# An attention-plus-MLP kernel: the hand-written call order of its first four chunks replaced by one in which products and evictions are listed separately

## The chip, the cores and the metric

One core of one Trainium2 chip runs the whole program. The metric is the device time of one execution in microseconds, the median of several runs. A profile of one execution gives a row for every instruction of the five engines: TensorE (PE in the rows, its weight loads PEld), VectorE (DVE), ScalarE (ACT), GpSimd (POOL) and the queue that issues transfers (SP).

## The reference

```python
# q, k, v: (4, 8, 768, 64); sort_net: (4, 8, 8, 8); w_in: (512, 2048); w_out: (2048, 512)
P = sort_net
for _ in range(5):
    P = exp(P - max(P, -1)); P = P / sum(P, -1); P = P / sum(P, -2)
k_sorted = einsum('bhij,bhjcd->bhicd', P, k_blocks)      # 8 blocks of 96 rows
v_sorted = einsum('bhij,bhjcd->bhicd', P, v_blocks)
s = q_blocks @ k_sorted^T / 8
attn = softmax(s) @ v_sorted                             # per block of 96 queries
x = attn reshaped to (3072, 512)
h = x @ w_in
out = (h * cos(h)) @ w_out                               # (3072, 512) float32
```

## The kernel before

All matrix operands are bfloat16, PSUM and the output float32. Each engine works through its own instruction list in order, so the order in which the Python calls are made is the schedule: it is written out by hand, call by call.

**Chunks and units.** The 3072 tokens are eight chunks `n` of 384 tokens. A chunk is four units `u` of 96 queries, one block of one batch element with its eight heads. Chunks 0 to 3 belong to the first group of two batch elements, 4 to 7 to the second.

**The head.** The five rounds of normalisation (`rounds`) run on DVE and ACT. Two small products (`block`) turn the result into matrices `bds[0]` and `bdv` (`spread`, DVE) that mix the key and value rows. `kp` makes sorted keys of the first batch element in PSUM tiles of 16 column steps, and `k_place` moves them to `kTs`, `half=0` for the blocks of chunk 0 and `half=1` for those of chunk 1. `kxp` (POOL) copies keys of chunk 1 to the other rows. `v_permute` (POOL) reorders value columns, `v0` makes eight of the 64 sorted value columns, `v0e` moves them to `vS[0]`.

**A unit of attention.** `s_ps` scores on PE, `s_max` and `s_sub` on DVE, `expo` the exponential on ACT, `p_ps` the transpose of the probabilities on PE with its eviction `p_ev`, `av_products` on PE, `av_norm` on DVE (a reciprocal and a multiplication), `x_ps` the transpose of the result on PE and its eviction `x_ev` to `xT`. From chunk 2 on the scores are `qk_half`, `qk` or a `batch`, and part of the transposes are DMAs on the SP queue.

**The MLP.** `up` makes two of the 16 blocks of h (eight products of 384 columns), ACT takes the cosine, DVE multiplies. `down` accumulates 16 products of 512 columns to 128 output rows. Chunk 0 does this in half chunks and quarters: `up_four(h, g, part)` needs only units 0 and 1 for `h=0` and 2 and 3 for `h=1`; `cos_four`, `gate_four`, and `down_four(ts, q)`.

**Other work in between.** `ks`/`kse` sort the keys of batch element 1, `v_sort_b` its values (64 columns in eight calls), `k_sort_g` and `v_sort_g` those of the second group (into `kT2` and `vS[1]`, which lies in `pair`), `q_products`/`q_place_half` transpose the queries.

**Buffers that tie the lists together.** PSUM holds three tiles named `big` of two banks and two named `acc` of one, taken in turn; a product waits until the tile three (or two) allocations back has been evicted. Every large load goes through the one queue that POOL issues: `load`, `load_pair`, `load_q`, `load_w_in`, `load_w_out`.

`keep_warm` puts out products of zeros on PE, as `fill=` of some calls as well. The calls of before, in the first stretch, joined to lines:

```python
kp(2, *B); kp(0, *B); v_permute x4; k_place(2, A, 1); k_place(2, V, 0); kp(1, *B); k_place(0, A, 0)
blocks.append(block(...)); k_place(1, V, 0); k_place(1, A, 1); values_matrix(); k_place(0, A, 1)
s_ps(0, 0, fill=3); v0(4, *C); s_max(0, 0); v0(0, *B); v0e(4, A); s_sub(0, 0); s_ps(0, 3); ...
```

Units of chunk 0 come in the order 0, 3, 1, 2, those of chunk 1 in the order 1, 0, 3, 2. All eight `v_sort_b` of batch element 1 stand between the eight `up` of chunk 1.

Of the kernel before, what the change touches and what calls it, by code (L numbers as in the profile page):

```python
# [18 lines left out]
def kernel(  # L19
# [15 lines left out]
    nc = tc.nc  # L35
# [214 lines left out]
    keep_warm(14, big.tile([128, 512], FP32, name="idle", tag="big"))  # L250
# [80 lines left out]
    def idle(times):  # L331
        keep_warm(times, big.tile([128, 512], FP32, name="idle", tag="big"))
# [64 lines left out]
    blocks = [block([pick[:]])]  # L397
    spread(bds[0], blocks[0], xs=slice(H, 2 * H))

    def values_matrix():  # L400
        spread(bdv, blocks[1], xs=slice(0, H))
        spread(bds[0], blocks[0], xs=slice(0, H))
        spread(bdv, blocks[1], xs=slice(H, 2 * H))
# [197 lines left out]
    def p_hold(n, u):  # L601
        hold(pT[n, u])
# [14 lines left out]
    def av_products(n, u, fill=0):  # L617
# [5 lines left out]
        pt = pT.pop((n, u)).rearrange("p a c -> p (a c)")  # L623
# [123 lines left out]
    def kp(t, pool, tag, fill=0):  # L747
        o = ps["k", t] = pool.tile([128, 16, 2 * NB], FP32, name="ks", tag=tag)
        keep_warm(fill, o[:, :8].rearrange("p t n -> p (t n)"))
        for z in range(16):  # L750
            k_products(o, z, t * 16 + z, slice(0, 128),
                       bds[0][:, H:].rearrange("p x i -> p (x i)"))

    def k_place(t, eng, half=None):
        lo, hi = (0, nb) if half is None else (half * IC, half * IC + IC)
        o = ps["k", t]
        copy_on(
            eng, kT[0].rearrange("p z (h i) t -> p z h i t", i=nb)[
                :, ::2, :, lo:hi, t * 16:t * 16 + 16],
# [134 lines left out]
    wz = iter(range(40, D, 4))  # L894
    kz = iter(range(6, 12))

    def k_next():
        k_sort_g(next(kz) * 4, A, *C)

    def w_next(eng=A, pool=None, tag="acc"):  # L900
        v_sort_g(next(wz), 4, eng, pool or acc, tag)

    kp(2, *B)
    kp(0, *B)
    v_permute(slice(0, 64), 32, False, 8, 40)
    v_permute(slice(0, 64), 40, False, 8, 48)
    v_permute(slice(0, 64), 48, False, 8, 56)
    v_permute(slice(0, 64), 56, False, 8, 64)
    k_place(2, A, 1)
    k_place(2, V, 0)  # L910
    kp(1, *B)
    k_place(0, A, 0)
    blocks.append(block([pick[:, :, z * PB:(z + 1) * PB] for z in (1, 0)]))
    k_place(1, V, 0)
    k_place(1, A, 1)
    values_matrix()
    k_place(0, A, 1)
    s_ps(0, 0, fill=3)
    v0(4, *C)
    s_max(0, 0)  # L920
    v0(0, *B)
    v0e(4, A)
    s_sub(0, 0)
    s_ps(0, 3)
    v0e(0, A)
    v0(5, *C)
    s_max(0, 3)
    load_w_out(0)
    v0e(5, A)
    s_ps(0, 1)  # L930
    load_w_out(1)
    load_w_out(2)
    load_w_out(3)
    v0(6, *C)
    ones(0)
    expo(0, 0, True)
    s_ps(0, 2)
    s_sub(0, 3)
    v0(1, *C)
    v0e(6, A)  # L940
    s_max(0, 1)
    expo(0, 3, True)
    v0(3, *B, fill=2)
    s_sub(0, 1)
    v0e(1, A)
    p_ps(0, 0, *C, fill=2)
    v0e(3, A)
    s_max(0, 2)
    v0(7, *C)
    expo(0, 1, True)  # L950
    kxp(2)
    v0(2, *B, fill=1)
    p_ev(0, 0, V)
    v0e(7, A)
    s_sub(0, 2)
    kxp(0)
    p_ps(0, 1, *C)
    v0e(2, A)
    p_ps(0, 3, *C)
    p_ev(0, 1, V)  # L960
    expo(0, 2, True)
    kxp(1)
    av_products(0, 0)
    z_turned(1)
    av_norm(0, 0, True)
    av_products(0, 1)
    p_ev(0, 3, A)
    p_ps(0, 2, *C)
    av_norm(0, 1, True)
    x_ps(0, 0, *B)  # L970
    load(kbuf, 0, kin_d[1])
    p_ev(0, 2, A)
    load(vbuf, 64, vin_d[1])
    picks(pick_pair, (2, 3))
    av_products(0, 3, fill=2)
    av_norm(0, 3, True)
    x_ps(0, 1, *C)
    x_ev(0, 0, A)
    av_products(0, 2)
    q_products(1, 0, 0, 16, *C)  # L980
    x_ev(0, 1, A)
    av_norm(0, 2, True)
    x_ps(0, 3, *B)
    q_place_half(1, 0, 1, A)
    up_four(0, 0, 0)
    z_vperm()
    up_four(0, 0, 1)
# [267 lines left out]
```

## Time and profile before

| | |
|---|---|
| median of 3 runs | 232.1 us (231.99 to 232.11) |
| the profiled execution's own time | 231.61 us |
| its span, first to last instruction | 229.8 us |
| PE busy | 220.8 us (96%) |
| DVE busy | 170.8 us (74%) |
| ACT busy | 154.4 us (67%) |
| POOL busy | 96.1 us (42%) |

The span leaves 1.8 us of the execution outside. Busy time of PE is not PE at its peak: products are pipelined, and a row lasts longer than the distance to the next. The chain of work that ended last, in order of time, gives the distance.

### The profile page before, as it was taken

How to read it: one execution, taken by the hardware profiler on the slowest of the kernel's cores; microseconds unless marked ns; L12 is line 12 of the kernel's file. 1: busy time of each engine (PE TensorE's matmuls, PEld its weight loads, DVE VectorE, ACT ScalarE, POOL GpSimd, SP SyncE). 2: the span in 40 equal slices, each digit the busy share in tenths (PEclk: the TensorE clock that was granted, in tenths of full speed). 3: DMA queues.
4: the chain of work that ended last, by engine and by line, in shares of the span. 5: the costliest groups of instructions: out<-in, count | busy, mean ns of one | idle time of the engine just before them, and what ended most of it. 6: DMA issues, size and time to landing. Idle time of an engine off the chain costs nothing.

```text
span 229.8 us, 5513 instructions
## 1 busy us (share of the span) xinstructions
PE 220.8 (96%) x2245; PEld 138.7 (60%) x2268; DVE 170.8 (74%) x291; ACT 154.4 (67%) x207; POOL 96.1 (42%) x121
## 2 busy tenths in 40 slices
PE   8788999999999999999999999999999999999994
PEld 3378898567765566655665456655655565556554
DVE  6769968978698778868489977987699769646700
ACT  5659877777889858797688466736674667716521
POOL 7999999399950197943609000800000000000000
PEclk9999999999999999999999999999999999999999
DMA  6999999994999799667979939964924440351012
GB/s 83 225 187 207 202 206 236 195 227 148 124 124 191 171 139 148 118 135 146 162 118 163 135 74 148 210 98 81 206 92 80 90 160 0 69 147 46 0 46 94
DMA packets 67833, 31.21 MB, mean 136 GB/s; under 512 B 56416, under 2 KB 63200, under 8 KB 67552
## 3 DMA queue, kind: packets, MB, share of 16 engines
q0 software_dynamic: 24048, 13.64, 43.3%
q1 hardware_dynamic: 43472, 17.02, 35.1%
q8 instruction: 18, 0.29, 0.5%
q10 hardware_dynamic: 288, 0.20, 0.3%
q14 instruction: 7, 0.06, 0.1%
HBM read 27.27 MB, written 6.29 MB: 146 GB/s over the span
## 4 chain that ended last, share of the span: by engine, by line
PE 90%; DVE 3%; POOL 2%; issue 1%; ACT 1%; POOLq 0%; ACTq 0%
PE h L672 32%; PE o L697 30%; PE h L860 5%; PE o L881 4%; PE av L628 4%; PE sc L441 3%; PE ks L408 2%; PE o L1219 2%; PE pps L838 1%; PE sc L507 1%; PE xps L659 1%; PE vs L785 1%; PE vs L452 1%; PE qps L268 1%; PE xps L847 1%
## 5 line engine op out<-in xcount | busy, mean ns | idle before, releaser
L672 PE MATMUL h<-xT,w_in_t 128*128 128x384 bf16 x448 | 78.4, 326 | 0.1
L697 PE MATMUL o<-w_out_t,gg 128*128 128x512 bf16 x303 | 73.7, 379 | 1.0 <-issue 0.3
L676 ACT ACTIVATE c<-h,half_pi 128x768 f32<-128x768 f32 x56 | 50.5, 902 | 26.0 <-PE h L672 25.0
L680 DVE TENSOR_TENSOR gg<-c,h 128x768 bf16<-128x768 f32 x56 | 52.7, 949 | 19.5 <-ACT c L676 19.5
L672 PEld LDWEIGHTS <-w_in_t 128*128 128x128 bf16 x448 | 42.2, 98 | 26.3 <-DVE xT L259 0.6
L697 PEld LDWEIGHTS <-gg 128*128 128x128 bf16 x320 | 29.0, 99 | 28.3
L573 ACT ACTIVATE p_buf<-s 96x768 bf16<-96x768 f32 x32 | 26.6, 843 | 5.2 <-DVE s L494 4.0
L179 POOL COPY vperm<-kv 64x768 bf16<-64x768 bf16 (+2 forms) x12 | 28.4, 2416 | 3.9 <-DMA kv<-in_v_dram 3.9
L494 DVE TENSOR_TENSOR s<-sc,mx 96x384 f32<-96x384 f32 (+1 forms) x33 | 24.3, 735 | 1.6
L492 DVE TENSOR_REDUCE mx<-sc 96x4 f32<-96x384 f32 (+1 forms) x33 | 24.0, 729 | 0.2 <-PE sc L507 0.2
L641 DVE TENSOR_TENSOR xn<-av,r 96x512 bf16<-96x512 f32 x32 | 22.0, 687 | 1.1
L129 POOL DMA_DIRECT2D kv<-in_q_dram x24 | 16.0, 676 | 0.7 <-issue 0.7
L257 ACT COPY kv<-o 128x512 f32<-128x512 f32 (+2 forms) x10 | 5.2, 524 | 14.1 <-PE o L697 11.5
L257 ACT CAST kTs<-ks 128x512 bf16<-128x512 f32 (+1 forms) x18 | 11.0, 630 | 5.3 <-PE ks L408 4.4
L639 DVE RECIPROCAL r<-av 96x8 f32<-96x8 f32 x32 | 6.4, 199 | 9.6 <-PE av L628 9.1
L129 POOL DMA_DIRECT2D q_mem<-in_q_dram x16 | 10.7, 687 | 2.0 <-DMA kv<-in_v_dram 1.5
L881 PE MATMUL o<-w_out_t,gg 128*128 128x512 bf16 x45 | 11.2, 379 | 0.2
L259 DVE COPY kv<-o 128x512 f32<-128x512 f32 (+1 forms) x5 | 3.1, 612 | 11.1 <-PE o L1219 8.5
L860 PE MATMUL h<-xT,w_in_t 128*128 128x192 bf16 x128 | 11.1, 246 | 0.0
L441 PE MATMUL sc<-kTs,q_turned 128*128 128x96 bf16 x152 | 11.1, 206 | 0.0
L599 POOL CAST held<-q_turned 96x1 f32<-96x1 bf16 x2 | 0.4, 184 | 24.3 <-DMA q_turned<-q_mem 16.3
L860 PEld LDWEIGHTS <-w_in_t 128*128 128x128 bf16 x128 | 10.5, 98 | 0.0
(134 smaller groups left out, 285.6 us busy)
## 6 DMA issues: line engine op xcount, KB each, us to landing
out_dram<-kv SPq DMA_DIRECT2D x12, 256.0 KB, 2.7
out_dram<-o_s SPq DMA_DIRECT2D x10, 256.0 KB, 3.5
w_in_t<-in_moe_w_in_dram POOLq DMA_DIRECT2D x4, 512.0 KB, 11.7
w_out_t<-in_moe_w_out_dram POOLq DMA_DIRECT2D x4, 512.0 KB, 12.3
kv<-in_k_dram POOLq DMA_DIRECT2D x2, 768.0 KB, 9.8
kv<-in_v_dram POOLq DMA_DIRECT2D x2, 768.0 KB, 12.9
pair<-in_k_dram POOLq DMA_DIRECT2D x2, 768.0 KB, 12.3
kv<-in_v_dram POOLq DMA_DIRECT2D x6, 256.0 KB, 5.3
```

The source lines that it names most:

```text
L129: nc.gpsimd.dma_start(out=q_heads[:, i, :, e], in_=src[:, ih * IC + i, :, e])
L179: nc.gpsimd.tensor_copy(dst, src)
L492: nc.vector.reduce_max(mx[:], scv, axis=AX.X)
L494: nc.vector.tensor_tensor(s, scv, mx.to_broadcast(list(s.shape)), op=ALU.subtract)
L573: nc.scalar.activation(p[:, :, :blk], s_t.pop((n, u)).rearrange("p e h c -> p (e h) c"), AF.Exp, scale=scale)
L641: nc.vector.tensor_tensor(xn.rearrange("p h e d -> p e h d"), avv[:, :, :, :D], r.to_broadcast([blk, 2, H2, D]), op=ALU.mult)
L672: nc.tensor.matmul(h[:, f2, :w], w_in_t[:, kk, f * 128:(f + 1) * 128], xT[n][:, kk], start=(kk == 0), stop=(kk == KC - 1))
L676: nc.scalar.activation(c[:], h[:, :, :w], AF.Sin, bias=half_pi[:, 0:1])
L680: nc.vector.tensor_tensor(gt[n, fp // 2][:, f:f + 2], c[:], h[:, :, :w], op=ALU.mult)
L697: nc.tensor.matmul(o[:], gt[n, f // 4][:, f % 4, ts * 128:(ts + 1) * 128], w_out_t[:, f, :], start=(f == 0), stop=(f == FC - 1))
L860: nc.tensor.matmul(o[:, part, f2 * w:(f2 + 1) * w], w_in_t[:, kk, f * 128:(f + 1) * 128], xT[0][:, kk, h * w:(h + 1) * w], start=(kk == 0) ...
L881: nc.tensor.matmul(out_ps[ts][:], gt[0, q][:, f % 4, ts * 128:(ts + 1) * 128], w_out_t[:, f, :], start=(f == 0), stop=(f == FC - 1))
```

## The change

The calls from the first keys to the output layer of chunk 3 are listed anew. What was one call with a product and its eviction becomes two, so that each engine's list has an order of its own: `uh`/`uc`/`ug` for `up`, `dn`/`dc` for `down` (in quarters), `qs`/`qr` and `qs2`/`qr2` for `qk_half` and `qk`, `bt`/`be` for `batch`, `xp`/`xe`, `kg`/`kge`, `vg`/`vge`, `vb`/`vbe`. The instructions are the same, but for three things: the first keys are made in four PSUM tiles (columns 16 to 24, 32 to 48, 0 to 16, 24 to 32) instead of three; the ones beside the values are set by DVE instead of POOL; the zero products have 256 columns instead of 512, twice as many of those in `idle` and at the start, and other `fill` counts in between.

The units of chunk 0 come in the order 0, 1, 2, 3, those of chunk 1 in the order 2, 3, 1, 0. Several evictions change engine.

```diff
-    keep_warm(14, big.tile([128, 512], FP32, name="idle", tag="big"))
+    keep_warm(28, big.tile([128, 512], FP32, name="idle", tag="big"), 256)
...
-    blocks = [block([pick[:]])]
+    blocks = [block([pick[:]]), block([pick[:, :, z * PB:(z + 1) * PB] for z in (1, 0)])]
     spread(bds[0], blocks[0], xs=slice(H, 2 * H))
...
+    nc.vector.memset(vS[0][:, :, D:D + 1], 1.0)
...
-    def kp(t, pool, tag, fill=0):
-        o = ps["k", t] = pool.tile([128, 16, 2 * NB], FP32, name="ks", tag=tag)
+    def kp(c, n, pool, tag, fill=0):
+        o = ps["k", c] = pool.tile([128, n, 2 * NB], FP32, name="ks", tag=tag)
...
+    def uh(n, fp):
+        h = ps["h", n, fp] = big.tile([128, 2, 512], FP32, name="h", tag="big")
...
+    def uc(n, fp):
+        c = ps["c", n, fp] = cosp.tile([128, 2, TC], FP32, name="c", tag="c")
...
+    def vb(b, d0, nd, pool, tag):
+        o = ps["vb", b, d0] = pool.tile([128, nd, 2 * NB], FP32, name="vs", tag=tag)
...
+    def vbe(b, d0, nd, eng):
+        copy_on(
+            eng, vS[0][:, b * 2 * NB:(b + 1) * 2 * NB, d0:d0 + nd],
+            ps.pop(("vb", b, d0))[:blk].rearrange("p t n -> p n t"))
...
+    def dn(n, ts, q):
+        if q == 0:
+            out_ps[n, ts] = acc.tile([128, Dm], FP32, name="o", tag="acc")
...
```

The new list, calls joined to lines (B is a `big` tile, C an `acc` tile, V is DVE, A is ACT), from the first keys to chunk 1's first `uh`:

```python
kp(16, 8, *B); k_place(16, A, 0); kp(32, 16, *B); k_place(32, V, 0); kp(0, 16, *B)
v_permute(40..48); k_place(16, A, 1); k_place(0, A, 0); v_permute(48..56); kp(24, 8, *C)
k_place(24, V, 0); k_place(24, V, 1); v0(0, *C); v_permute(32..40); s_ps(0, 0); k_place(32, A, 1)
k_place(0, A, 1); v0e(0, A); kxp(0); v0(5, *B); v0e(5, A); v0(2, *C); s_max(0, 0); s_sub(0, 0)
s_ps(0, 1); v0(6, *C); s_max(0, 1); v0e(2, A); v0e(6, A); s_ps(0, 2); s_ps(0, 3); expo(0, 0)
s_max(0, 2); v0(3, *C); v0e(3, A); v_permute(56..64); p_ps(0, 0, *C, fill=1); v0(1, *C); s_sub(0, 1)
picks(pick_pair); p_ev(0, 0, A); s_max(0, 3); expo(0, 1); v0e(1, A); v0(4, *C); v0e(4, A)
v0(7, *B, fill=1); v0e(7, A); p_ps(0, 1, *C, fill=1); load(vbuf); s_sub(0, 2); s_sub(0, 3)
z_turned(1); load(kbuf); load_w_out(0); av_products(0, 0, fill=2); p_ev(0, 1, V)
av_products(0, 1, fill=1); av_norm(0, 0); expo(0, 2); p_ps(0, 2, *B); last = block([pick_pair[:]], *C)
av_norm(0, 1); expo(0, 3); p_ps(0, 3, *B); p_ev(0, 3, V); load_w_out(1); kxp(1); p_ev(0, 2, A)
x_ps(0, 0, *C); x_ps(0, 1, *B); x_ev(0, 1, V); kxp(2); av_products(0, 2, fill=1); load_w_out(2)
x_ev(0, 0, A); av_products(0, 3); av_norm(0, 2); spread(bds[1], last); up_four(0, 3, 0) ...
x_ps(0, 2) ... up_four(0, 1) ... x_ps(0, 3); q_products(1, 0); q_products(1, 1) ... up_four(0, 0)
up_four(0, 2) ... up_four(1, 1) ... ks(4, *C); up_four(1, 0) ... s_ps(1, 2); ks(0, *C); up_four(1, 2)
down_four(0, 0); s_ps(1, 3); down_four(2, 0); up_four(1, 3); down_four(0, 1) ... down_four(2, 3)
down_out(0, A); s_max(1, 0); down_out(2, A); s_sub(1, 0); kse(5, V); ks(1, *B); kse(1, V)
vb(1, 8, 8, *C); vbe(.., A); p_ps(1, 2, *B); ks(2, *C); p_ev(1, 2, V); vb(1, 32, 8, *B); vbe(.., V)
vb(1, 24, 8, *B); p_ps(1, 3, *C); p_ev(1, 3, V); p_ps(1, 1, *B); kse(2, A); vbe(24, A); vb(1, 48, 8, *C)
ks(3, *B); vb(1, 56, 8, *C); expo(1, 0); p_ev(1, 1, V); av_products(1, 2); vbe(48, A); av_norm(1, 2)
kse(3, A); p_ps(1, 0, *B); p_ev(1, 0, V); down_four(1, 0); av_products(1, 3); av_norm(1, 3); kg(16, *B)
av_products(1, 0); av_norm(1, 0); kge(16, A); down_four(1, 1); x_ps(1, 2, *B); down_four(1, 2)
x_ev(1, 2, A); vbe(56, V); av_products(1, 1); x_ps(1, 0, *B); down_four(1, 3); x_ev(1, 0, A)
x_ps(1, 3, *B); av_norm(1, 1); vb(1, 40, 8, *C); down_out(1, V); x_ps(1, 1, *B); x_ev(1, 3, A)
vbe(40, V); x_ev(1, 1, A); vb(1, 16, 8, *B); vbe(16, V); q_products(2, 0, *B); q_products(2, 1, *B)
q_place_half(2, 0, 0, V); q_place_half(2, 1, 0, V); uh(1, 4); uc(1, 4) ...
```

After that the list goes on in the same manner to the end of chunk 3's `dn`; `kg(24)` and `kg(40)` now stand between the `uh` of chunk 1, the loads of the second group's values and queries are issued earlier, and nothing is changed from the transposes of `q` for chunk 6 on.

838 lines of the change are left out of this document (566 added, 272 removed).

## Prediction

> **What bounds the kernel now.** I read the page first, then PE's busy time by stretches, then the chain of work that ended last in order of time, then the waits and the engines' rows in the stretch where the chain leaves PE.
>
> ```profile
> span 229.8 us, 5513 instructions
> PE 220.8 (96%) x2245; PEld 138.7 (60%) x2268; DVE 170.8 (74%) x291; ACT 154.4 (67%) x207; POOL 96.1 (42%) x121
> ```
>
> ```profile
> 12.05:27.75 15.70, 14.31 (x302) 1.00 1.23 201
> 27.75:56.40 28.65, 28.49 (x395) 1.00 1.04 207
> 56.40:84.06 27.66, 27.45 (x309) 1.00 0.99 146
> ```
>
> (Stretch, its length, PE busy and instructions, granted clock, DMA share, GB/s.) 96% alone would not prove it, because a product's row outlasts the distance to the next. The chain, which counts from start to start, does (start, length, what):
>
> ```profile
> 12.09 0.36 PE bl L386 x8
> 12.75 1.56 PE ks L408 x48
> 14.31 0.51 PE bl L386 x16
> 14.82 0.34 PE sc L246
> 15.59 0.35 PE sc L804 x16
> 15.96 0.96 DVE mx L824
> 19.49 0.84 PE vs L785 x8
> 20.34 0.22 PE vs L246
> 26.98 0.50 PE qps L268 x16
> 27.75 3.30 PE h L860 x40
> 48.36 0.36 PE pps L838 x8
> 48.72 0.26 PE av L628 x8
> 50.47 0.17 PE xps L847 x4
> 52.12 0.86 PE o L881 x4
> 58.28 1.30 PE h L672 x8
> 59.59 0.25 PE vs L452 x8
> 205.82 10.40 PE h L672 x64
> ```
>
> Eight `h` products take 1.30 us at 58.28 and 64 take 10.40 at 205.82: 0.1625 us each in both, whatever lies between. From 27.75 us on, PE runs at one rate, and the two stretches leave it 0.16 and 0.21 us idle. All the products there stay in the new list, so after 27.75 nothing can be won but some 0.3 us; it can only be lost. The stretch from 12 to 27.75 is different: the chain passes through DVE and zero products (L246), and PE is idle 15.70 − 14.31 = 1.4 us beside the zeros.
>
> **The change part by part.**
>
> *First keys.* A row of the waits (total, times, longest) and DVE's rows in order of time (start, length, line, what, count):
>
> ```profile
> DVE kTs L259 <- ACT kTs L257: 1.3, 1, 1.3
> 14.03 1.29 DVE L259 CAST kTs<-ks 128x512 bf16<-128x512 f32 x2 [1.34 <-ACT kTs L257]
> 17.82 0.94 DVE L824 TENSOR_REDUCE mx<-sc 96x8 f32<-96x768 f32 x1
> 18.80 0.95 DVE L828 TENSOR_TENSOR s<-sc,mx 96x768 f32<-96x768 f32 x1
> 22.39 0.54 DVE L259 COPY pT<-pps 96x768 bf16<-96x768 bf16 x1
> 24.75 0.69 DVE L641 TENSOR_TENSOR xn<-av,r 96x512 bf16<-96x512 f32 x1
> 25.35 0.19 DVE L639 RECIPROCAL r<-av 96x8 f32<-96x8 f32 x1
> 28.03 0.34 DVE L259 COPY xT<-xps 128x384 bf16<-128x384 bf16 x1
> ```
>
> Before, DVE waits 1.3 us for ACT's half of the same keys, and the first scores start at 15.59. In the new list the halves that share an engine follow one another. PE: first `block` to 12.45, second (0.51) to 12.96, the 48 `kp` products (1.56) to 14.52, `v0(0)` (0.84, from 19.49) to 15.36. DVE: three spreads to 13.5, the ones (not shown on DVE; POOL's row for them is 0.73 us, a small DVE memset 0.06, and both fit), `k_place(32)` to 14.5 or 14.8, `k_place(24, V, 0)`, half as large, by 15.2. So the scores start at about 15.36 and DVE's first `s_max` at 15.8, 0.16 earlier, with PE having done useful work where zeros stood (14.82 to 15.59).
>
> *DVE's chain through units 0 and 1.* From there DVE is busy without a break, and its list decides when `up_four(0, 3)` can start. A subtraction right after its own maximum starts 0.98 after it (17.82 to 18.80), an independent pass 0.87 after the one ahead (16.95 to 17.82: the step before that row). Before, the pairs stood the first way, with `p_ev(0, 0)` and `p_ev(0, 1)` among them. Now one pair does, and `p_ev(0, 0)` goes to ACT. The sum: eight passes 8 × 0.87 + 0.11 = 7.1; `p_ev(0, 1)` 0.53; two `av_norm` at 0.87 (0.69 and 0.19, overlapping by a little) 1.74; `p_ev(0, 3)` 0.53; `x_ev(0, 1)` 0.34; together 10.3, so 15.8 + 10.3 = 26.1. PE and ACT keep up: ACT's `expo(0, 3)` would end near 24.5, PE's `av(0, 3)` near 26.05. `up_four` starts at 26.15 instead of 27.75: 1.6 earlier. Not all is won. Before had by then done the `q_products` (0.50) and one more `x_ps` (0.17); after has done `last` (0.30). Net 1.6 − 0.67 + 0.30 = **1.2 us gained**. The zero products in this stretch go from 6 × 0.22 + 4 × 0.11 = 1.8 us to 0.22 + 6 × 0.11 = 0.9; that is part of the 1.2, not beside it. Those before 12 us keep their sum of columns and cover waits for rows that do not move: 0.
>
> *POOL and the load queue.* The keys of batch element 1 (`load(kbuf)`) now have to be there for `ks(4)`, which stands behind five `up_four` calls.
>
> ```profile
> 12.76 0.82 POOL L119 DMA_DIRECT2D q_mem<-in_q_dram  x1
> 13.94 5.87 POOL L179 COPY vperm<-kv 64x768 bf16<-64x768 bf16 x4 [0.36 <-DMA kv<-in_v_dram]
> 26.03 1.40 POOL L142 MEMSET q_turned<- 64x1568 bf16 x1
> 29.04 0.54 POOL L88 DMA_DIRECT2D kv<-in_k_dram  x1
> 29.57 0.55 POOL L88 DMA_DIRECT2D kv<-in_v_dram  x1
> kv<-in_k_dram POOLq DMA_DIRECT2D x1, 768.0 KB, 11.7
> kv<-in_v_dram POOLq DMA_DIRECT2D x1, 768.0 KB, 14.7
> DMA to landing us min/median/max: 5.1/7.3/14.1
> ```
>
> (The last row is that of `load_q`, L119; the maximum is the second one, issued at 12.76.) Landings: `load_q(1)` 12.76 + 14.1 = 26.9, keys 29.04 + 11.7 = 40.7, values 29.57 + 14.7 = 44.3. Both were queued, so the values, of the same size as the keys, took 3.6 us of the queue. In the new list the values are issued near 23 (four `v_permute` at 1.47 from 13.94, and some 3 us for `kxp(0)` and `picks`) and the keys near 26.5 (two such memsets of `z_turned`, 2.8, later), both before the queue has come to them: values land at 26.9 + 3.6 = 30.5, keys at 34.1. PE comes to `ks(4)` after five `up_four` at 1.32 (3.30 / 40 × 16), two `x_ps` at 0.17 and two `q_products` at 0.50: 26.15 + 7.95 = 34.1. There is no margin, so the head can hardly win more than 1.2 to 1.4 us, and each us by which the keys are late costs one. `w_out` follows in four parts at 2.4 us by their size (36.5 to 43.7), each ahead of its `down_four`; `load_w_out(3)` waits on POOL behind the `v_permute` that waits for the values, to about 34, and the queue has work till then. Of the other moved POOL work, `kxp(1)` and `kxp(2)` end near 30, four us ahead of the scores that read them: 0.
>
> *Chunk 1's attention.* Seven `v_sort_b` leave the shelter of the `up` calls, and four of their evictions, all four `p_ev(1, ·)`, `down_out(1)` and one more `kse` are now DVE's. From `ks(1)` to the first `uh` PE has eleven small sorts at 0.25 (2.75; as 59.59), four `p_ps` at 0.36, four `av` at 0.26, four `down_four` at 0.86, four `x_ps` at 0.17 and two `q_products` at 0.50: 10.4 us. DVE has six casts at 0.65 (half of 1.29), four `p_ev` at 0.53, four norms at 0.87 and `down_out`, a cast of the same size, 0.65: 10.1 us, with four `q_place` like `p_ev` behind. Two full lists with waits on each other: at best nothing is lost, at worst each of the eighteen small sorts and transposes waits 0.15, 2.7 us. Going through the buffers in turn I find three waits of 0.05 to 0.1 and one of 0.2 before `uh(1, 4)`; I take **0.35 lost**.
>
> *The rest to chunk 3.* The up stretches have the same sums: in chunk 1, DVE has 8 × 0.87 for `ug` and four half passes against eight `uh` at 1.30. ACT loses eight casts and gets two. The loads of chunk 3's queries are issued earlier, and POOL's reorderings too. The transposes stay with the engines that had them. Bounds: −0.3 (idle that goes) to +1 (one wait of a `dn` for a late `kge`); I take **0.15 lost**. Extra calls (`dc`, `be`) cost nothing, since no instruction is added.
>
> The sum: −1.2 + 0.35 + 0.15 = −0.7 us. Against the profiled execution's 231.61 (span 229.8 and 1.8 around it) that is 230.9; the median of the runs stands 0.5 above it, so **231.4 us**.
>
> **A rule of the Trainium skill.** The clock is first a matter of rows: the zero products at the start are issued 0.42 us apart, later ones of the same size 0.22 (20.34).
>
> ```profile
> 1.83 0.15 PEld L246 LDWEIGHTS <-warm 128*128 128x128 bf16 x1 [0.28 <-issue]
> 2.25 0.15 PEld L246 LDWEIGHTS <-warm 128*128 128x128 bf16 x1 [0.28 <-issue]
> ```
>
> The granted clock reads 1.00 all the while, so it does not show this. The Trainium skill, "TensorE: Matmul & The Clock Gate" (Part 1), says that PE runs at half rate until it has been busy for a window of about 3.4 us and falls back after an idle one, and (Part 4) that transposes don't count as busy; by it, halving the zeros amid transposes speaks against the change. The trace agrees with the start, and no row shows a fall after 12 us.
>
> **The rivals.**
>
> 1. *The head's gain is given back (no change).* Chunk 1's attention loses 1 to 1.5 us instead of 0.35. For it: DVE's 10.1 against PE's 10.4. Against: before, DVE was 74% busy and PE hardly waited. 232.1 us.
> 2. *Slower: DVE's list in chunk 1's attention sets the pace.* Place: `ks(1)` to `uh(1, 4)`; price up to 2.7 us; it decides from 1.7 us on (1.2 won and 0.5 of measurement). −1.2 + 2.2 + 0.15: 233.2 us.
> 3. *The keys are late at `ks(4)`.* POOL's list comes to the key load after 30.5, say behind a `z_turned` that waits. Each us costs one; 1.5 late gives 232.9.
> 4. *The clock falls.* If PE went on at the rate of the start from 23 to 26 us, about 2 us of products would take 4, part of it under DVE's chain: 1.5 us, 232.9. Against it: the longest idle of PE that I find there is some 0.5 us.
> 5. *More is won*, up to 230.3: no wait in chunk 1, and PE's 0.3 idle gone.
>
> **How the numbers follow.** A measurement of this kernel tells 0.2% (0.46 us) from nothing. Forecast (−1.4 to −0.47) 0.47; rival 5 0.05; rival 1 0.21; rival 2 0.17; rival 3 0.06; rival 4 0.04. Faster 0.52, same 0.21, slower 0.27. The likeliest one's own range is 230.7 to 231.65; the range with both signs runs from 230.4 to 233.2, leaving out 3% below and some 12% above.
>
> **What the profile of the changed kernel would show.** Right: no wait of DVE `kTs` for ACT `kTs`; first scores near 15.4; the first `h` near 26.1; keys landed by 34.4 and no wait of PE `ks` for a DMA; PE's distance per `h` still 0.1625; PE idle between 47 and 58 under 0.6 us. Wrong: a first `h` after 27, a PE row waiting for `kv<-in_k_dram`, waits of PE for DVE's `vS`, `pT` or `xT` adding to over 1.2 us, or products at twice the distance.

## The result and the profile after

The changed kernel takes 235.41 us (median; 235.08 to 235.82), the kernel before beside it 232.06 us: a ratio of 1.0140, 95% interval 1.0123 to 1.0157. It is 3.35 us slower; 0.7 us faster was forecast, and the range ended at 233.2. The profiled execution is one of 235.82 us, with a span of 234.1 us, 4.3 us longer than before. One or two runs each of e10, e16, e17 and e18 below fell in a slower state and are left out of their medians and ratios.

Two lines of the page, the timeline at the places that the prediction named, and the longest waits of TensorE (engine, line, what it waited for: us in total, times, longest; those before 13 us and those under 0.3 us are left out). `...` stands for rows left out.

```profile
span 234.1 us, 5573 instructions
...
PE 220.2 (94%) x2267; PEld 140.8 (60%) x2287; DVE 177.9 (76%) x302; ACT 148.2 (63%) x199; POOL 95.2 (41%) x120
```

```profile
15.26 0.40 PE L803 MATMUL sc<-kTs,q_turned 64*128 64x64 bf16 x16
...
15.70 0.95 DVE L823 TENSOR_REDUCE mx<-sc 96x8 f32<-96x768 f32 x1 [0.29 <-PE sc L803]
...
26.20 1.49 PE L859 MATMUL h<-xT,w_in_t 128*128 128x192 bf16 x16
...
35.93 0.41 PE L407 MATMUL ks<-bd,kv 128*128 128x64 bf16 x8 [1.68 <-DMA kv<-in_k_dram]
```

```profile
PE av L627 <- DMA pT<-p_buf: 2.2, 2, 1.7
PE ks L407 <- DMA kv<-in_k_dram: 1.7, 1, 1.7
...
PE h L671 <- DMA xT<-xn: 0.5, 1, 0.5
PE h L898 <- DVE vS L259: 0.3, 1, 0.3
```

In this execution the head is what was forecast: scores at 15.26 (15.36), first maximum at 15.70 (15.8), first up projection at 26.20 (26.15). Two waits that were not there before take all of it back and more: 1.7 us for chunk 1's keys at `ks(4)`, and 1.7 us at `av(2,2)`, deep in chunk 2, for the transpose of `p(2,2)`. The chain of waits (start, us, what) puts both on a transfer:

```profile
27.02 8.86 DMA kv<-in_k_dram
35.93 0.41 PE ks L407 x8
...
78.28 6.89 DMA pT<-p_buf
85.22 0.43 PE av L627 x8
```

The keys were issued at 27.02 (26.5 in the prediction) and landed at 35.88 (34.1). The 6.89 us of the transpose stand beside 2.84 and 4.12 us for the two issued ahead of it. GpSimd's timeline over the same time shows what is new:

```profile
73.23 2.88 POOL L179 COPY vperm<-kv 128x1536 bf16<-128x1536 bf16 x1 [9.84 <-DMA kv<-in_v_dram]
76.05 5.34 POOL L129 DMA_DIRECT2D q_mem<-in_q_dram  x8
81.37 1.87 POOL L137 MEMSET q_mem<- 96x1024 bf16 x2
```

The eight small loads of chunk 4's queries (`load_q(4)`) are issued from 76.05 to 81.4, right over the transpose that TensorE waits for, which is issued at 78.28.

### The profile page after: what moved, and what is told of

Read it like the earlier page. It is cut to its first block, busy times and chain, and to the rows that moved or that the text cites. A ratio compares the mean times of both kernels' runs of the same rounds, so it can differ in the third digit from the quotient of the medians.

```text
span 234.1 us, 5573 instructions
## 1 busy us (share of the span) xinstructions
PE 220.2 (94%) x2267; PEld 140.8 (60%) x2287; DVE 177.9 (76%) x302; ACT 148.2 (63%) x199; POOL 95.2 (41%) x120
## 4 chain that ended last, share of the span: by engine, by line
PE 68%; DMA 17%; POOL 5%; ACT 5%; issue 3%; DVE 1%; POOLq 0%; ACTq 0%
PE h L671 18%; PE h L898 13%; PE o L696 12%; PE o L996 7%; DMA kv<-in_v_dram 5%; DMA pT<-p_buf 4%; PE o L880 4%; DMA kv<-in_k_dram 4%; PE av L627 2%; PE sc L440 2%; POOL vperm L179 2%; DMA vperm<-p_buf 2%; ACT p_buf L572 2%; PE h L859 2%; DMA xT<-xn 2%
## 5 line engine op out<-in xcount | busy, mean ns | idle before, releaser
L671 PE MATMUL h<-xT,w_in_t 128*128 128x384 bf16 x256 | 43.2, 326 | 0.5 <-DMA xT<-xn 0.5
L696 PE MATMUL o<-w_out_t,gg 128*128 128x512 bf16 x169 | 39.9, 379 | 0.4
L675 ACT ACTIVATE c<-h,half_pi 128x768 f32<-128x768 f32 x32 | 28.8, 901 | 16.1 <-PE h L671 16.1
L671 PEld LDWEIGHTS <-w_in_t 128*128 128x128 bf16 x256 | 24.6, 98 | 17.0 <-issue 1.3
L996 PE MATMUL o<-w_out_t,gg 128*128 128x512 bf16 x135 | 34.2, 379 | 0.6 <-issue 0.2
L898 PE MATMUL h<-xT,w_in_t 128*128 128x384 bf16 x192 | 33.5, 326 | 0.3 <-DVE vS L259 0.3
L898 PEld LDWEIGHTS <-w_in_t 128*128 128x128 bf16 x192 | 18.2, 98 | 11.2 <-issue 0.2
L257 ACT CAST kTs<-ks 128x512 bf16<-128x512 f32 (+2 forms) x15 | 8.8, 612 | 4.6 <-PE ks L407 4.6
```

The source lines that it names most:

```text
L671: nc.tensor.matmul(h[:, f2, :w], w_in_t[:, kk, f * 128:(f + 1) * 128], xT[n][:, kk], start=(kk == 0), stop=(kk == KC - 1))
L675: nc.scalar.activation(c[:], h[:, :, :w], AF.Sin, bias=half_pi[:, 0:1])
L696: nc.tensor.matmul(o[:], gt[n, f // 4][:, f % 4, ts * 128:(ts + 1) * 128], w_out_t[:, f, :], start=(f == 0), stop=(f == FC - 1))
L898: nc.tensor.matmul(h[:, f2, :TC], w_in_t[:, kk, f * 128:(f + 1) * 128], xT[n][:, kk], start=(kk == 0), stop=(kk == KC - 1))
L996: nc.tensor.matmul(out_ps[n, ts][:], gt[n, q][:, f % 4, ts * 128:(ts + 1) * 128], w_out_t[:, f, :], start=(f == 0), stop=(f == FC - 1))
```

## The experiments

Each kernel was timed beside the kernel before, which took 232.03 to 232.18 us; ratios are to it, with their 95% intervals. Edits are against the changed kernel where nothing else is said, and shortened.

### Where do the 3.35 us lie: first four kernels

*e1_keys_first*: the keys' load listed earlier, ahead of `kp(24)`.

```
     v_permute(slice(0, 64), 40, False, 8, 48)
+    load(kbuf, 0, kin_d[1])
     k_place(16, A, 1)
...
     kp(24, 8, *C)
...
     z_turned(1)
-    load(kbuf, 0, kin_d[1])
+    z_vperm()
...
     up_four(0, 0, 0)
-    z_vperm()
```

> The changed kernel with its key load issued before the value load (near 16 us instead of 27.0) and with z_vperm moved up on POOL to where the value load would keep POOL waiting. Theory (the loss is PE waiting for transfers, 1.85 us of it at ks(4) for the keys): the keys land near 31, PE's wait of 1.7 us at ks(4) goes, but the four w_out loads keep their landings (38.2 to 46.1) and take back up to 0.8 us of it: 234.3 us, 1.1 less than the changed kernel's 235.4. Rival A (the wait only moves to the values' reorderings or to w_out): 235.2 to 235.6. Rival B (the order of evictions in chunk 1's attention is what costs, the wait at ks(4) only stands where PE would wait anyway): 235.4.

*e2_q4_later*: chunk 4's queries loaded later.

```
     v_permute(slice(0, 128), 48, True, 16, 64)
-    load_q(4)
     dn(1, 0, 2)
     zeros_between(4)
...
     v_permute(slice(0, 128), 16, True, 16, 32)
+    load_q(4)
```

> The changed kernel with load_q(4) issued behind zeros_between(4) and the v_permute of columns 16 to 32 (near 80.7 us instead of 76.05). Theory (the eight query loads run between the transposes of p(2,2) and make that DMA take 6.9 us where others take 2.8 to 4.1; PE waits 1.8 us for it at av(2,2)): the transpose lands near 82, the wait falls under 0.3: 233.7 us, 1.7 less. Rival A (the transpose is late of itself, for the queue or the exponential before it): the landing stays near 85 and the time at 235.4. Rival B (the loads then delay the transposes of q for chunk 4 or the reorderings): 234.5 to 235.5.

*e3_both*: both edits.

> Both edits, of the keys and of load_q(4), in the changed kernel. Theory (independent waits, on one list of PE): the sum, 1.1 and 1.7 less: 232.6 us. Rival (evictions set the pace in between, so that what is won ahead of 50 us is lost before 83): no less than 233.7, that is the second edit alone.

*e4_head_only*: the kernel before with the new head; its loads, and its calls from the first up projection on, stay as before, but for `x_ps(0, 2)` and `x_ps(0, 3)`, which are exchanged.

```
-    kp(2, *B)
-    kp(0, *B)
...
+    kp(16, 8, *B)
+    k_place(16, A, 0)
+    kp(32, 16, *B)
...
     up_four(0, 0, 0)
```

> The kernel before with the new head alone: first keys in four tiles, units in the order 0, 1, 2, 3, p_ev(0,0) on ACT, ones on DVE, fewer zero products; loads in the order of before (w_out, then keys and values), and from up_four(0,0) on the calls of before, with x_ps(0,2) and x_ps(0,3) exchanged. Theory (the head wins what the prediction worked out, since the changed kernel's first h starts at 26.20 instead of 27.75): 1.0 to 1.2 less than before: 230.9 to 231.1 us. Rival (the gain is given back by later waits whatever the loads' order): 232.1 within 0.4.

Measured: e1 250.05 us, ratio 1.0772 [1.0754, 1.0790]; e2 233.80 us, 1.0082 [1.0053, 1.0111]; e3 249.23 us, 1.0741 [1.0717, 1.0764]; e4 233.12 us, 1.0041 [1.0028, 1.0054].

e1 and e3 say nothing on the theory: the load stood ahead of `kp(24)`, products that still needed the old keys, TensorE waited 16.1 us there for the new ones, and what was to be tested was buried. What follows from e2: its wait at `av(2,2)` is gone from the list of waits, and 1.6 us of the medians (1.35 by the ratios) with it. The transposes of `p(2, ·)` land after 3.75, 3.52 and 2.83 us there, and GpSimd issues the small loads at 80.95, 0.1 us after the last of them has landed. That is the forecast of the theory (233.7), and the same pair is seen in all the profiles. In the nine in which the small loads are issued beside it (the change, e1, e5, e8, e9, e10, e14, e17 and e18), the transpose of `p(2,2)`, the third of three, lands after 5.48 to 6.89 us; in the eleven others, the kernel before among them, after 2.79 to 2.89. TensorE's wait for it at `av(2,2)` is 1.7 us in the change, 1.2 in e8, 1.5 in e9, 1.8 in e14, 1.0 in e17 and 1.3 in e18, only 0.4 in e10; in e2, e11, e15, e16 and e19 there is none over 0.25 us. So the cause of that wait is shown. What it is worth is another matter, taken up under "Why the prediction was wrong". GpSimd's timeline in e2:

```profile
78.17 2.84 POOL L179 COPY vperm<-kv 128x1536 bf16<-128x1536 bf16 x1
80.95 5.34 POOL L129 DMA_DIRECT2D q_mem<-in_q_dram  x8
```

e4 lost its gain at once, in a wait that the change itself does not have:

```profile
PE h L859 <- DVE gg L871: 1.2, 1, 1.2
```

ScalarE's copy of chunk 1's queries stands ahead of the first cosine in that listing, the first gate is late, and an up projection waits for its PSUM buffer.

### Are the keys late because of what is ahead of them?

*e5_keys_first* and *e6_keys_q4*: the keys behind `kp(24)`, alone and with e2's edit. *e7_head_mended*: e4 with the first cosine in order. *e8_ks_later*: no load moved, TensorE reaches `ks(4)` later.

```
# e5, e6
     kp(24, 8, *C)
+    load(kbuf, 0, kin_d[1])
...
     z_turned(1)
-    load(kbuf, 0, kin_d[1])
+    z_vperm()
...
     up_four(0, 0, 0)
-    z_vperm()
# e7 (against e4)
     up_four(0, 0, 1)
+    cos_four(0, 0)
     x_ps(0, 2, *C)
     x_ev(0, 2, V)
+    gate_four(0, 0)
...
-    cos_four(0, 0)
...
-    gate_four(0, 0)
# e8
-    ks(4, *C)
     up_four(1, 0, 0)
     up_four(1, 0, 1)
+    ks(4, *C)
+    kse(4, A)
     cos_four(1, 0)
-    kse(4, A)
+    up_four(1, 2, 0)
     s_ps(1, 2)
...
     kse(0, V)
-    up_four(1, 2, 0)
```

> The changed kernel with one edit on GpSimd: the load of chunk 1's keys is issued right behind the products that read the old keys (kp(24)) instead of behind the values, and the zeroing of vperm takes its old place. TensorE's, VectorE's and ScalarE's lists stay as they are. Theory (the keys land late because the values run ahead of them in the same queue): the keys land near 31, ks(4) waits 0 us instead of 1.7 to 1.85, w_out's four parts land where they did (38.2, 40.8, 43.6, 46.1), so that a few tenths come back at the first output products: 233.8 to 234.4 us against 235.4. Rival (it is all the bytes ahead of w_out that count, whichever come first): TensorE runs into w_out's landings instead and the time stays within 0.4 of 235.4. Rival 3 (the load so early slows w_in's tail and the first up projection): a wait for w_in or q(1) of over 0.5 us shows at 26 to 30 us.

> The changed kernel with both edits: chunk 1's keys issued ahead of its values, and chunk 4's queries (load_q(4)) issued behind v_permute(0:128, 16..32) as in e2. Theory (the two waits are separate places, 50 us apart, and add up): e5's gain and e2's gain of 1.6 us together, 232.2 to 232.8 us, the time of before within 0.3%. Rival (a wait taken away at 34 us is given back at w_out's landings or in chunk 1's attention): 233.4 to 233.9, no better than e2. If the head's gain of 1.2 us that shows at the first up projection is whole and nothing else is lost, it ends below before, near 231.0.

> The kernel before with the new head alone, as in e4_head_only, but the first cosine (cos_four(0,0)) stands ahead of ScalarE's copy of chunk 1's queries and its gate right behind x_ev(0,2) on VectorE, so that the 1.2 us for which an up projection waited for the gate at 31 us should be gone. Theory (the head's gain is real and only the calls behind it lost it): 233.1 less 1.33, 231.8 us, with 0.4 to 0.6 off from before at every later mark. Rival (the head is no gain at all, units 2 and 3 are as late as before and set the end of the head): 232.5 to 233.1, with the wait at some other up projection. If the whole 1.2 us of the prediction is there: 230.9.

> The changed kernel with the loads as they are and four calls moved: TensorE does up_four(1,0) (16 products, 1.3 us) ahead of ks(4) and up_four(1,2) ahead of s_ps(1,2) and ks(0), ScalarE evicts ks(4) ahead of cos_four(1,0). No byte is moved earlier or later. Theory (only the order of PE's work against a landing at 35.9): the wait at ks(4) shrinks from 1.85 to about 0.5, 234.1 us (233.8 to 234.6). Rival (w_out's landing at 38.2 to 46.1 is the next limit, or s_ps(1,2) waits for the eviction): 1 us is lost at the first output products or the scores and the time stays at 235.1 to 235.6.

Measured: e5 250.28 us, 1.0795 [1.0773, 1.0817]; e6 248.94 us, 1.0725 [1.0697, 1.0753]; e7 231.95 us, 0.9994 [0.9984, 1.0004]; e8 236.17 us, 1.0191 [1.0170, 1.0212].

e5 misses again, and e6 with it, for another reason. TensorE's longest wait in e5:

```profile
PE vs L784 <- DMA kv<-in_k_dram: 16.7, 1, 16.7
```

It is at `v0(0)`, products on *values*. Values and keys are two halves of one tile, and `v_cols` takes 128 columns of a view with 96 real ones (`vv = kv[:, :128 * D]`): the spare columns lie in the first third of the keys' half. So the keys cannot be loaded before `v0(0)` to `v0(3)` have read those columns, and `v0(0)`, listed behind the load, waited for it.

e7 ties with the kernel before: mended, the new head is worth nothing there. In its profile the first up projection starts 0.92 us earlier than before and the second to eighth gates come 0.15 to 0.22 earlier.

e8 is the first to show a reason. Its TensorE list before 34 us is that of the change, and yet:

```profile
PE av L627 <- DMA pT<-p_buf: 1.7, 2, 1.2
PE vs L784 <- issue: 1.4, 1, 1.4
```

The chain of waits of e8 over its first 19 us, and of the change:

```profile
2.72 13.25 DMA kv<-in_v_dram
...
16.02 1.49 POOL vperm L179
```

```profile
2.74 11.53 DMA kv<-in_v_dram
...
14.32 1.74 POOL vperm L179 x2
```

Chunk 0's values landed at 15.97 in e8 and at 14.27 in the change: one transfer with one issue time, 1.7 us apart. `v0(0)` follows wherever the values land after TensorE is ready at 14.45. (That wait is put down to "issue" in e8 and to an earlier product in e2; the landing is the event that fits in both.) Laid beside one another, six of the nine kernels with the change's head, its order of `v0(0)` and its loads up to there (the other three, e10, e16 and e18, have landings at 15.27 to 15.38 and a first up projection at 27.15 to 27.34, like e2):

| kernel | values land | `v0(0)` | first scores | first up | TensorE ready for `ks(4)` | keys land |
|---|---|---|---|---|---|---|
| e15 | 13.82 | 14.43 | 15.23 | 26.18 | 37.13 (moved) | 35.15 |
| e17 | 14.05 | 14.47 | 15.28 | 26.22 | 34.10 | 27.63 (cut) |
| change | 14.27 | 14.45 | 15.26 | 26.20 | 34.08 | 35.88 |
| e2 | 15.28 | 15.37 | 16.18 | 27.17 | 35.06 | 34.83 |
| e19 | 15.64 | 15.73 | 16.57 | 27.54 | 35.42 | 33.52 (half) |
| e8 | 15.97 | 16.06 | 16.90 | 27.86 | 37.33 (moved) | 36.53 |

Over the nineteen profiled executions of the change and the experiments, one of each kernel, the values land between 13.82 and 15.97, at 15.27 in the median. It is not the lists that make the difference: e5 and e6 are the same up to 80 us and have 15.59 and 14.38, e17 and e16 have 14.05 and 15.38. Before, in the one execution that was profiled, they landed at 13.89, the scores stood first, and no product on the values ran before 15.85.

e8 does not decide what it was made for. With its late values TensorE would have come to `ks(4)` near 36.0 in the change's order (an estimate: 37.33 less 1.3 for the 16 products moved ahead), only 0.5 us before the keys, so that there was little wait to hide. Its time, 236.17, lies above the ranges of both.

### The loads exchanged, and the scores first

*e9_v0_behind*: `v0(0)` behind `s_ps(0, 0)`. *e10_swap*: keys and values exchanged in the change's places. *e11_three*: both, and e2's edit. *e12_head_v0*: e7 with e9's edit.

```
# e9, e11, e12
-    v0(0, *C)
     v_permute(slice(0, 64), 32, False, 8, 40)
     s_ps(0, 0)
+    v0(0, *C)
# e10, e11
-    load(vbuf, 64, vin_d[1])
+    load(kbuf, 0, kin_d[1])
...
-    load(kbuf, 0, kin_d[1])
+    load(vbuf, 64, vin_d[1])
```

> The changed kernel with one call moved: v0(0), the first products on chunk 0's values, stands behind the first scores s_ps(0,0) instead of ahead of them. Theory (a third cost, which the profiled execution of the change happens not to show): the values land between 13.9 and 16.0 us from one execution to the next, and v0(0) follows at once wherever they land after 14.4 (14.27 and 14.45 in the change, 14.68 and 14.77 in e7, 15.28 and 15.37 in e2, 15.97 and 16.06 in e8), so that the scores and all behind them slide. Over the executions seen, the landings lie 0.6 us past 14.4 in the mean. With the scores first, TensorE waits instead for the copies of kT at 14.9 to 15.2 in every execution, which costs 0.3 to 0.8, but the first scores start at 15.3 at the latest whatever the values do. So 235.2 us (234.7 to 235.6) and a first maximum on VectorE between 15.4 and 15.9. Rival (the landing does not matter, since the fills behind it take up what it costs): slower by the 0.3 to 0.8, 235.7 to 236.2.

> The changed kernel with two loads exchanged in their places on GpSimd: chunk 1's keys are issued where its values were (23.4 us) and the values where the keys were (27.0). e1 and e5 issued the keys at 16.7 and 18.4 and did not test this, since v0(0) to v0(3) read 128 columns of a 96-wide strided view and so touch the keys' buffer behind them: in both traces TensorE stood at v0(0) until the keys had landed, 16 us later. Both places here are behind all of these products. Theory (the keys are late because the values run ahead of them): the keys land at 30.5 to 32, ks(4) waits for nothing, the values land near 36, and w_out where it did: 1.0 to 1.85 us less than the change, 233.5 to 234.4. Rival (what counts is the total of bytes ahead of w_out): the output products wait from 38 us on and the time stays within 0.4 of 235.4. Against the theory, too: GpSimd's v_permute(64:128, 48) stands ahead of load_w_out(3) and now waits for the values until 36; w_out's last part is then issued near 39 and could land after 46.1.

> The changed kernel with the three repairs together: the keys ahead of the values as in e10, chunk 4's queries later as in e2, v0(0) behind the first scores as in e9. Theory (three separate places at 14, 34 and 83 us, which add up): 235.4 less 1.4, 1.6 and 0.2, so 232.2 us (231.6 to 232.8). Rival (what is given back at one is lost at the next): no better than e2, 233.4 to 234.

> e7_head_mended (the kernel before with the new head alone and the cosine in order, 231.95 us) with v0(0) behind the first scores. Theory (the head's gain depends on where the values land): 231.6 us (231.1 to 231.9), below the kernel before, and the runs closer together than e7's 231.1 to 232.2. Rival (the head is bound by units 2 and 3 and its fills, not by the first scores): 232.0 to 232.6, no better than e7.

Measured: e9 235.68 us, 1.0157 [1.0137, 1.0177]; e10 237.02 us, 1.0209 [1.0196, 1.0223]; e11 236.84 us, 1.0207 [1.0189, 1.0226]; e12 232.22 us, 1.0002 [0.9993, 1.0012]. All four miss the theory's time; e12 comes out at its rival's, and e10 and e11 are slower than their rivals have it.

In e9 and e12 the scores start at 15.17 and 15.14 whatever the values do, and nothing is gained: e9's first up projection starts at 28.29, with the values at 15.51, and e12's at 26.46, with the values at 14.32. The scores are not the only thing in the head that hangs on the values; GpSimd's `v_permute` calls, and through them the other `v0`, start when the values land too.

e10 does what it says: the keys land at 30.97 and `ks(4)` waits for nothing. It is still 1.6 us slower than the change. GpSimd's timeline in e10, and under it the same calls in the change:

```profile
34.86 2.87 POOL L179 COPY vperm<-kv 64x1536 bf16<-64x1536 bf16 x1 [2.38 <-DMA kv<-in_v_dram]
37.67 0.74 POOL L164 DMA_DIRECT2D w_out_t<-in_moe_w_out_dram  x1
...
48.09 2.82 POOL L179 COPY vperm<-kv 64x1536 bf16<-64x1536 bf16 x1
```

```profile
31.58 2.87 POOL L179 COPY vperm<-kv 64x1536 bf16<-64x1536 bf16 x1
34.38 0.74 POOL L164 DMA_DIRECT2D w_out_t<-in_moe_w_out_dram  x1
...
44.80 2.90 POOL L179 COPY vperm<-kv 64x1536 bf16<-64x1536 bf16 x1
```

The values, now second, land at 34.74; the first `v_permute` of chunk 1 waits for them, and all that GpSimd issues or copies behind it is 3.3 us later, to the end of chunk 1's attention. Some 0.95 of that is not the exchange: chunk 0's values landed at 15.27 in this execution, and the first of the two loads is issued at 24.34 instead of 23.39. TensorE stands for the reordering from 49.6 to 51.0:

```profile
PE vs L983 <- POOL vperm L179: 1.4, 1, 1.4
```

So the wait was moved from the keys to the values' reordering. In e11 the same place costs 0.7, and another 1.2 goes to queries of a later chunk.

### One wait or two?

*e14_old_head*: the change with the old head. *e15_ks_behind_up*: e2 with `ks(4)` behind `up_four(1,0)` and `up_four(1,2)`.

```
# e14
-    kp(16, 8, *B)
-    k_place(16, A, 0)
     kp(32, 16, *B)
-    k_place(32, V, 0)
     kp(0, 16, *B)
...
     spread(bds[1], last)
# e15
-    ks(4, *C)
     up_four(1, 0, 0)
     up_four(1, 0, 1)
     cos_four(1, 0)
+    up_four(1, 2, 0)
+    up_four(1, 2, 1)
+    ks(4, *C)
     kse(4, A)
+    gate_four(1, 0)
+    cos_four(1, 2)
+    up_four(1, 3, 0)
     s_ps(1, 2)
...
```

> The changed kernel with the head of the kernel before (three first key tiles in its order, scores of units 0 and 3 first, the values' matrix behind them), and from the first up projection on the calls and loads of the change. Theory (the time at the end of ks(4) is the keys' landing, which no faster head moves; the head's gain is spent waiting there): the first up projection starts 1 to 1.5 us later than in the change, the wait at ks(4) shrinks by as much, and the time stays within 0.5 us of the change, 235.0 to 235.9. Rival (the head's 1.2 us is a gain of its own, on top of which the keys cost 1.85): 236.4 to 236.9, with the whole wait still there.

> e2 (the changed kernel with chunk 4's queries later, 233.8 us) with no load moved and TensorE's list changed between 34 and 44 us: up_four(1,0) and up_four(1,2), 32 products of 82 ns or 2.6 us, go ahead of ks(4), and the scores of unit 2 behind the first half of up_four(1,3). TensorE then reaches ks(4) at 36.7 where the keys land at 35.9 to 36.8. Theory (the wait for the keys is a cost by itself and can be hidden by order alone): no wait at ks(4), 1.2 to 1.85 us less, 232.0 to 232.6. Rival (the scores come later by so much that chunk 1's maxima, exponentials and transposes end later, or the output products meet w_out's landings at 38.2 to 46): a wait of the same size shows at the scores, the output products or av(1,2), and the time stays at 233.4 to 234.2.

Measured: e14 235.61 us, 1.0147 [1.0113, 1.0181]; e15 234.76 us, 1.0109 [1.0089, 1.0130].

e14 is the theory's: first up projection at 28.80, 2.6 us later than in the change's profile; TensorE ready for `ks(4)` at 36.68, keys at 35.95, no wait; and the time is that of the change. What a fast head wins, it spends at `ks(4)`; what a slow head loses, it does not pay twice. e15 is the rival's in kind, and slower than the rival's 234.2: no wait at `ks(4)`, but the second scores wait for a PSUM buffer that DVE has not yet read:

```profile
41.04 0.51 PE L440 MATMUL sc<-kTs,q_turned 128*128 128x96 bf16 x8 [1.42 <-DVE s L827]
```

### Bytes instead of order

*e16_keys_split_q4* and *e17_keys_split*: the sixth of the keys that `ks(4)` reads goes first, with and without e2's edit. *e18_half_keys* and *e19_half_keys_q4*: half of chunk 1's key rows are not loaded.

```
# e16, e17
     kp(24, 8, *C)
+    nc.gpsimd.dma_start(out=kbuf[:64, 4 * CD // 6:5 * CD // 6], in_=kin_d[1][:, 4 * CD // 6:5 * CD // 6])
...
-    load(kbuf, 0, kin_d[1])
+    for lo, hi in ((0, 4), (5, 6)):
+        nc.gpsimd.dma_start(
+            out=kbuf[:64, lo * CD // 6:hi * CD // 6], in_=kin_d[1][:, lo * CD // 6:hi * CD // 6])
# e18, e19
-    load(kbuf, 0, kin_d[1])
+    nc.gpsimd.dma_start(out=kbuf[:32], in_=kin_d[1][:32])
```

> e2 (chunk 4's queries later, 233.8 us) with the load of chunk 1's keys cut by columns: the sixth that ks(4) reads (columns 4096 to 5120, which no v0 touches) is issued right behind kp(24), ahead of the values, 131 KB; the other five sixths go in two pieces where the whole stood. TensorE's, VectorE's and ScalarE's lists stay, the bytes stay, the values and w_out come 0.7 us later at most. Theory (the wait at ks(4) is a cost by itself in the change, and the head's gain shows as soon as the keys are there): the sixth lands before 30, ks(4) starts when TensorE reaches it (34.0 if the first values land before 14.4), the rest lands near 35.5 to 36 and ks(0), due 2.1 us after ks(4), does not wait; 232.0 to 232.8 us. Rival (what is saved at ks(4) is lost at the output products, which meet w_out at 38.9 and later, or GpSimd, 1 us longer with two more issues, brings v_permute late as in e10): 233.4 to 234.2, with that wait in the trace.

> The changed kernel with the cut load of e16 alone; chunk 4's queries stay where the change has them. Theory (a wait of 1.85 us at ks(4), separate from the one of 1.6 to 1.8 at av(2,2)): 233.6 to 234.4 us against 235.4, no wait at ks(4), the wait at av(2,2) whole. Rival (given back at w_out or on GpSimd): 235.0 to 235.8.

> The changed kernel with half the bytes of chunk 1's keys left out: rows 32 to 64 are not loaded and stay zero (part of chunk 1's scores is wrong by that), 0.39 MB less in the queue between the values and w_out; every engine's list is the change's. Theory (the load queue from 23 to 46 us is the bound that the change runs into, at the keys first and at w_out next): keys land near 33.8 and w_out's first part near 36.9, both before TensorE comes, no wait at ks(4) or the first output products; av(2,2) still waits. 233.4 to 234.2 us against 235.4. Rival (bytes are not the bound; some list is): 235.0 to 235.8.

> The same half of the keys left out, and chunk 4's queries later as in e2 (233.8 us). Theory (both costs of the change are taken away, so that what the head gives should show): 231.2 to 232.4 us, at or below the kernel before. Rival (what remains of the 1.7 us between e2 and the kernel before has another cause, in chunks 1 to 3): 232.9 to 233.9.

Measured: e16 234.54 us, 1.0109 [1.0085, 1.0134]; e17 234.73 us, 1.0117 [1.0089, 1.0145]; e18 234.36 us, 1.0088 [1.0058, 1.0118]; e19 233.85 us, 1.0060 [1.0036, 1.0083].

e16 is slower than both its forecasts, e17 lies between its two. e17's profile has the early values (14.05) and the whole head; TensorE comes to `ks(4)` at 34.10 and goes on. The next landing stops it:

```profile
34.10 0.40 PE L407 MATMUL ks<-bd,kv 128*128 128x64 bf16 x8
...
36.71 1.48 PE L859 MATMUL h<-xT,w_in_t 128*128 128x192 bf16 x16
39.17 1.02 PE L880 MATMUL o<-w_out_t,gg 128*128 128x512 bf16 x4 [0.97 <-ACT c L865]
```

ScalarE's cosine is named there, but `w_out`'s first part landed at 39.03, 0.14 us ahead of the product, so the wait is taken to be for it; in e16 the same wait (0.7 us, landing 39.85, product 39.98) is put down to `w_out`. Before, that part landed at 29.4 and was needed at 39.77; the change, which puts keys and values ahead of it, gave up those ten microseconds.

e18 takes bytes out and gains 1.05 us of the medians (1.2 by the ratios), about the least of the theory's 1.2 to 2.0; its profiled execution had late values (15.30), and no wait at `ks(4)` was there to be removed. With e2's edit the same bytes are worth nothing: e19 233.85, e2 233.80, and e19 is its rival's. The two costs of the change overlap, they do not add up. Of e19's list of waits these lie in the head and behind it:

```profile
PE vs L784 <- issue: 1.1, 1, 1.1
...
PE av L627 <- DMA pT<-p_buf: 0.5, 1, 0.5
PE h L671 <- DMA xT<-xn: 0.5, 1, 0.5
PE h L898 <- DVE vS L259: 0.3, 1, 0.3
```

The kernel before has one entry at the places behind the head, and none for a transpose:

```profile
PE o L697 <- issue: 0.3, 2, 0.2
```

## Why the prediction was wrong

Three terms of the sum failed: the head's −1.2, the 0 of the load queue, and the 0.15 of the rest to chunk 3.

**The head, −1.2.** The chain through VectorE was read rightly, and it came out to 0.1 us where the values land by 14.45, with some luck: the first maximum was 0.1 us earlier than forecast, and from there to the first up projection it took 10.5 us, where the terms of the sum make 10.2 (the prediction has 10.3). The 1.6 us were counted from 27.75, the chain's mark; the row of the first up projection before starts 0.16 us earlier:

```profile
27.59 3.47 PE L860 MATMUL h<-xT,w_in_t 128*128 128x192 bf16 x40
```

The step that failed is the one before the chain: "`v0(0)` (0.84, from 19.49) to 15.36" takes the values as landed, from one row of one execution (13.94, where GpSimd's first `v_permute` ended its wait). The new list puts a product on the values, due 0.6 us after that landing, ahead of the scores. By the prediction's own deductions (0.67 not yet done, 0.30 done early), a first up projection at 26.20 is worth 27.59 − 26.20 − 0.67 + 0.30 = 1.0 us, one at 27.17, with the values at 15.28, is worth 0.05, and 15.28 is about the median landing. That the new head brings nothing to the kernel before is what e7 and e12 measure (0.9994 and 1.0002). The late landing does not explain all of that: in their profiles, with values at 14.68 and 14.32, the second up projection starts 0.16 and 0.37 us earlier than before, and that lead lasts to 68 us; at 84 us it is gone, and at 111 us, the first up projection of chunk 3, they are 0.36 and 0.50 us behind, in calls that are the same in all three. e12 waits 0.5 us for transposes of `p` on that stretch and the kernel before not at all; but the one profile of the kernel before is of an execution 0.45 us faster than its median. So how much of the 1.2 us went with the landing, and how much behind the head, stays open.

**POOL and the load queue, 0.** The keys were forecast at 34.1 "with no margin", and rival 3 was given 0.06. They landed at 34.8 to 36.5 in the kernels that load them whole and in the change's order. The sum put each load behind the last and took 3.6 us for each of them; in the change `load_q(1)` landed at 28.25 instead of 26.9, the values at 31.01 (30.5) and the keys 4.87 us after them. In the profiled execution that costs 1.85 us (35.93 less the 34.08 at which TensorE was ready). It is not an addition to the loss of the head, though: with late values TensorE comes to `ks(4)` a microsecond later and finds the keys there (e2, e14). One of the two is lost in either profile (the change with its early values, e2 with its late ones), so that the 1.2 us do not get past 36 us.

**The rest to chunk 3, 0.15.** The prediction says that chunk 3's queries are loaded earlier and passes over chunk 4's; its upper bound, 1 us, is one wait for a late `kge`. It did not ask what the loads do to transfers that run beside them. With them beside it, the transpose of `p(2,2)` takes twice as long (5.48 to 6.89 us against 2.79 to 2.89), which is shown, and TensorE waits up to 1.8 us for it. Loading the queries later brings 1.6 us in e2 (1.35 by the ratios). But the same edit stands in four more pairs of kernels that differ in nothing else, and there the medians gain less by it: 1.3 (e5 to e6), 0.8 (e1 to e3), 0.5 (e18 to e19) and 0.2 us (e17 to e16), each known to some 0.8 us by the intervals. The gain does not follow the wait, either: e5's was 0.4 us at that place, e17's 1.0. So e2's figure is at the upper end of what this cost is worth.

**Chunk 1's attention, 0.35.** Near: between 47 and 58 us TensorE is idle for 0.11 us (under 0.6 was forecast). Behind it, where chunk 1's own `uh` begin, TensorE waits 0.27 for an eviction that VectorE now does. Rival 2 is not what happened.

**The clock, rival 4.** The granted clock reads 1.00 through the change's profile, and no products there stand at twice their distance: 16 `h` take 2.60 us at 63.12, the 0.1625 of before. What would have had to happen is to be seen in e5, where TensorE stood still for 16 us. Windows of e5 (stretch, length, busy time of PE, PEld, DVE, ACT, POOL with instruction counts, granted clock, DMA share, GB/s):

```profile
10.00:20.00 10.00, 3.94 (x97) 3.18 (x96) 3.67 (x16) 3.96 (x9) 7.99 (x9) 0.89 1.12 200
20.00:31.00 11.00, 0.00 (x0) 0.00 (x0) 0.00 (x0) 0.00 (x0) 4.85 (x7) 0.50 0.99 172
31.00:40.00 9.00, 8.25 (x149) 7.31 (x150) 7.09 (x9) 6.51 (x11) 1.56 (x2) 0.78 0.15 20
```

The clock is 0.50 while it stands and 0.78 in the mean of the 9 us after. The rule of the Trainium skill ("TensorE: Matmul & The Clock Gate", Part 1) that an idle window drops the rate to half agrees with that; the change has no idle as long.

**The sum.** Forecast (−0.7) and result (+3.35) lie 4.05 us apart. The head's 1.2 are absent: e7 and e12 gain nothing by the new head, and e14, the change with the old one, loses 0.2. Chunk 4's queries later and half of the keys left out take back 1.6 and 1.05 us alone, and 1.6 together (e19 against the change; 1.9 by the ratios). What is left, about 1.0 to 1.3 us, stays open. It is not one wait: in e19 it is entries of 0.3 to 0.5 us, the two largest each for a transpose, one of these at 207 us in calls that the change does not touch; in e2's profiled execution, the fastest of its eight, they are not there. Part of it may be chance, landings that differ from one execution to the next and a listing that has less room for them: e2's runs lie between 232.67 and 235.31, those of the kernel before beside it between 231.76 and 232.52. Part is not: the slowest of the last transposes `xT` (near 205 us in the change) lands after 3.66 to 4.36 us in each of the sixteen profiles with the change's list, and after 2.3 to 2.4 in the four with that of before, and in six of the sixteen TensorE waits 0.25 to 0.72 us for it. Neither reading was tested by itself.

No kernel here beats the one before; e7 and e12 equal it.

## What to carry to other kernels

When a new order puts work directly behind a transfer, the landing of one profiled execution is not a time to build on: ask how much earlier than its reader it lands, and treat less than a microsecond or two as none. A faster stretch is worth only what the next landing lets through (e14), so work out the arrival of everything due behind it, against all the bytes that the new order has put ahead. A load that is moved earlier is not free because nobody waits for it; look at which transfers it now runs beside, on other queues too. And try an edit in more than one kernel before its gain is booked: the one of e2 brought 1.6 us in one pair and 0.2 in another.

## What was not expected of the hardware

One load of 768 KB, issued at 2.7 us in every kernel, landed between 13.82 and 15.97. A DMA transpose of `p` that lands after 2.79 to 2.89 us in eleven profiles took 5.48 (e1) to 6.89 us (the change) in the nine in which eight loads of 48 KB were issued beside it. The slowest of the transposes `xT` near 205 us lands after 4.31 us in the change and in e19 and after 2.33 to 2.35 before and in e7, in calls that are the same; why was not found.
